# A linear-attention and expert-mixture kernel: another written-out order for its first third, and fewer planned waits for the x block sums

## The chip, the cores and the metric

The kernel runs on one core of a Trainium2 chip. The metric is the device time of one execution in microseconds (us). Three runs of the kernel before took 981.34, 982.95 and 984.04 us; their median, 982.95 us, is the time before. A separate execution was recorded by the profiler, and every duration below is from it.

The engines are called as the profile calls them: PE is TensorE (matrix products; PEld is its weight load), DVE is VectorE, ACT is ScalarE, POOL is GpSimd, and SP is SyncE, which here only starts transfers.

## The reference

```
phi(u) = where(u > 0, u, exp(u) - 1) + 1
kv  = sum over s of phi(k)[s,:] (outer) v[s,:]        per batch and head
x   = phi(q) @ kv / (phi(q) . sum_s phi(k) + 1e-6)    8 batches, 8 heads, 576 x 64
x   = x laid out as 4608 tokens x 512
P   = exp(x @ w_gate - max), 8 rounds of row and column normalisation
out = sum over e of P[:, e] * (relu(x @ w1[e]) @ w2[e])    8 experts, 512 -> 1024 -> 512
```

## The kernel before

**The front.** Sixteen groups of four heads (batch b, half g, group number 2b + g) go through linear attention. For each, k, q and v are loaded from POOL's queue into three buffers each (line 371). ACT takes exponentials (lines 381, 440), DVE forms phi (385, 389 for k, called Kt and Kmin here; 443, 447 for q), PE multiplies k by v (406), and the result is copied out of PSUM (kvz, 333 on DVE or 331 on ACT). PE transposes q (432), the copy out is qpT, PE forms denominators and numerators (463), and DVE writes the product to xT (491), which holds x transposed, 128 partitions by four chunks by 4608 tokens. After every four groups PE computes logits (508).

**The experts.** Tokens are cut in nine blocks of 512, experts and blocks in units. For expert 0 the first layer of the early blocks is plain (677) and the second too (925). From block 5 of expert 0 on, the first layer is a seven-product block scheme (803), whose operands are sums and differences: of x (`x_blocks`, lines 719 to 724), of w1 (the four W operations, 975), and for the second layer (1043) of w2 (the four T operations, 989) and of the hidden values (the four S operations, 1014). ACT and DVE turn products into hidden values (825 to 841). DVE adds second-layer products, scaled by the routing weights P_sb, to the output sums (1074). ACT and POOL do so for one product in seven (1081, 1084). Expert 0's outputs are scaled later, by P_sb, on ACT, DVE or POOL (893), because P_sb comes from eight rounds of normalisation (called Sinkhorn here, 534 to 565) that start only after the last logits. Each round holds a sum on DVE, a small product on PE (549) and a short step on DVE.

**x blocks.** For each of the nine token blocks three tasks form sums of x quarters: the first has two instructions, the others one. They may run on DVE or on POOL. The result is written to DRAM from SP's queue (736), the raw x too (704, 705), and experts 1 to 7 read both back (754). The first five blocks use one output buffer, acc6, as scratch.

**Weights.** w1 and w2 of an expert are loaded by POOL (306) into two buffers each, so w1 of expert 2 overwrites w1 of expert 0. w2 of experts 1 to 7 is one transfer of 1024 KB as stored, w1 two of 512 KB.

**What sets the order.** Nothing is emitted at once: every piece of work is a task with a cost for each engine that may run it, with priority, dependencies and buffer groups, added to a `_Plan`. `_Plan.run` then plays all tasks through a model of the engines and emits each when it is picked, so the plan decides only the order on each engine and which engine runs a task. The semaphore waits come from the data. At the start it follows a list, `_FRONT`, without choosing. A token such as `598g` is task 598 on POOL; p is PE, a is ACT, d is DVE, g is POOL, s is SP, m is a transfer's landing and n is bookkeeping. The list before has 1,506 tasks and ends at 1549p. After its end the model picks the earliest task, by priority. The order of PE's blocks in expert units is also a written chain. A task number is the same in both kernels, because tasks are added in the same sequence. Engines run their instructions in order, so an instruction that waits holds up all behind it on its engine, and on POOL that includes the issue of loads.

Tasks that the steps below name: 444g loads v of group 13, 450p is its k-v product; 472g and 478p are the same for group 14; 498g, 330g and 356g load q of 15, v of 9 and q of 10. 562g, 557g and 569g are x sums. 525p is the last logits product, 492p and 493d the last numerator and the last write of xT in the new order, 528d and 529p the sum and the product of the first Sinkhorn round, 552d its last step (P_sb). 737d to 740d are W, 741d to 744d are T of expert 0; 1011d to 1014d are T of expert 1, 1542d to 1545d T of expert 2. 598g and 1535g load w2 of experts 1 and 2, 1529g and 1531g load w1 of expert 2 in halves. 732g, 734g and 699g scale outputs of expert 0. 992p is the last block with w1 of expert 0, 1043d forms hidden values (841) in the first unit of expert 1, and 1044p is the PE block that reads what 1043d frees. 1405p, 1465p and 1468p are second-layer blocks at the end of expert 1 and the beginning of expert 2.

The lines that the change touches besides the list are the two places in `x_blocks` where a task is given dependencies on landed loads, and the lists that hold these.

Of the kernel before, what the change touches and what calls it, by code (L numbers as in the profile page):

```python
# [17 lines left out]
class _Plan:  # L18
# [121 lines left out]
    1n 108n 119n 601n 48s 49m 2p 3p 50g 51m 4p 0g 5p 6p 52g 53m 7p 8p 76g 77m 9p 78g 79m 10p 54a 11p 80g 81m 12p 13p  # L140
    14p 15p 126g 127m 16p 17p 18p 128g 129m 19p 20p 21p 61n 62a 63d 22p 23p 55d 24p 25p 26p 56d 27p 154g 155m 28p 29p
    30p 64d 130g 131m 31p 57n 32p 33p 109g 110m 58p 111g 112m 65p 59d 34p 66d 35p 36p 37p 89n 82a 60a 156g 157m 38p
    83d 90a 39p 67p 40p 84d 41p 68a 158g 159m 91d 85n 69p 92d 86p 70a 114g 115m 42p 87d 43p 44p 88d 93p 133d 116g
    117m 139n 132a 71a 45p 72p 94d 140a 73d 95p 182g 183m 134d 96a 74p 75d 97p 135n 184g 185m 98a 141d 136p 142d 99a
    186g 187m 46p 137d 143p 161d 138a 47p 160a 102p 144d 113n 120g 121m 602p 103d 145p 603p 146a 162d 100p 210g 211m
    604p 101d 147p 605p 163n 212g 213m 164p 214g 215m 118n 240g 241m 195n 167n 168a 169d 148a 170d 149a 171p 165d
    172d 166a 152p 173p 153d 606p 174a 608p 607d 150p 175p 151d 610p 188a 242g 243m 612p 609d 614p 176a 189d 123g
    124m 616p 615a 190d 196a 618p 197d 104g 105m 191n 177a 192p 198d 617d 611a 199p 193d 613a 620p 194d 122n 244g
    245m 200d 180p 621a 638n 622p 181d 619a 106g 107m 201p 217d 178p 202a 624p 179d 216a 223n 270g 271m 203p 225d
    639p 224a 218d 641p 268g 269m 219n 204a 226d 220p 205a 640d 300g 301m 227p 642d 643p 221a 228d 253n 246a 298g  # L150
    299m 645p 222d 247d 644a 206p 229p 207d 647p 230a 248d 646a 208p 125n 272g 273m 623p 209d 254a 302g 303m 231p
    255d 625p 630d 232a 249n 326g 327m 256d 233a 250p 328g 329m 632d 257p 648d 251a 281n 252a 628p 258d 282a 236p
    259p 237d 649p 260a 283d 234p 284d 261p 311n 274a 626p 235d 262a 651p 275d 650a 263a 285p 276d 354g 355m 266p
    653p 286d 384g 385m 277n 304a 267d 238p 312a 654d 278p 313d 305d 239a 627p 279a 306d 382g 383m 280a 652a 333d
    287p 330g 331m 264p 288a 672p 265d 307n 289p 314d 308p 290a 634d 339n 332a 674p 309d 310d 291a 315p 334d 412g
    413m 292p 659p 316d 358g 359m 340a 341d 356g 357m 317p 293d 629p 318a 414g 415m 342d 360a 294p 671n 319p 673d
    335n 660p 361d 320a 676p 675a 295d 496g 497m 388a 343p 416g 417m 336p 344d 636a 667d 321a 296p 386g 387m 337d
    367n 338d 657p 297a 362d 368a 322p 369d 345p 395n 323d 678p 346a 370d 677a 324p 347p 363n 325d 396a 658p 389d
    364p 348a 555d 349a 371p 665d 655p 390d 679a 562g 372d 661p 365a 425n 366a 419d 373p 352p 397d 374a 680p 353d
    418a 375p 427d 350p 472g 473m 682p 351d 391n 376a 442g 443m 662p 398d 426a 440g 441m 681d 392p 377a 470g 471m  # L160
    420d 556g 399p 428d 393a 656p 394a 400d 683a 380p 498g 499m 401p 381d 684p 402a 663d 378p 453n 403p 379d 421n
    686p 404a 685d 454a 422p 704n 687d 447d 429p 423a 444g 445m 405a 688p 557d 468g 469m 430d 705p 669a 500g 501m
    424d 503d 446a 406p 563g 431p 407d 707p 432a 448d 502a 408p 690p 409d 449n 708a 433p 455d 450p 434a 456d 706d
    435a 510n 457p 451d 689p 481n 458d 452a 505g 558s 559m 438p 696a 459p 439d 709p 460a 504d 436p 461p 437d 692p
    506n 462a 475d 710a 464p 693p 564d 463a 512d 565s 566m 691p 567s 568m 511a 465d 410p 474a 569g 513d 466p 711p
    483d 411a 467d 482a 514p 476d 507p 712a 515d 477n 713p 508a 570g 509a 715p 714d 516p 571d 484d 478p 517a 572s
    573m 560s 561m 698a 518p 479d 700a 717p 519a 574s 575m 694p 716a 480a 485p 520a 521p 486d 695p 522d 487p 719p
    583d 488a 576g 523p 720a 745n 489p 524d 721p 702a 718d 490a 494p 727p 491a 722p 577g 495d 728p 729a 492p 746p
    578g 493d 748p 584d 553n 747a 585d 735d 784g 725p 579s 580m 749a 586s 587m 741d 525p 581s 582m 742d 750p 743d
    526a 588s 589m 527n 737d 726p 751a 528d 785g 752p 733a 723p 753a 786g 754p 738d 739d 756p 842g 755a 787s 788m  # L170
    740d 529p 724p 757a 744d 530d 758p 531d 760p 759a 590g 843g 731a 591n 597n 554p 791n 761a 792p 794p 793a 762d
    766p 844g 795a 763d 532p 768p 767a 764d 592g 593m 798p 533d 772p 534d 594g 595m 789s 790m 845s 846m 847s 848m
    799a 769a 806p 1015s 1016m 773a 800p 802p 796p 776p 801d 797a 803d 807a 770p 777d 535p 810p 536d 812p 765d 808p
    813a 537d 804p 809a 816p 805a 778p 811a 850p 771a 596n 774p 779a 817d 851a 538p 814p 849n 539d 818p 815d 854p
    819a 900g 856p 855a 824p 820d 821d 864p 825a 866p 822d 865a 830p 775d 867a 901g 540d 870p 868p 871a 828p 869a
    902g 857a 874p 852p 872p 823d 853a 826p 873d 831a 860p 827d 541p 858p 861d 834p 875d 862p 835d 876p 863a 542d
    832p 958g 877a 859d 829a 908p 878d 836p 909a 879d 912p 1007d 907n 914p 913a 833d 922p 915a 959g 910p 880d 923a
    884p 543d 911a 918p 837a 960g 916p 882p 598g 599m 903s 904m 905s 906m 1072s 1073m 924p 961s 962m 883a 919d 928p
    963s 964m 925a 917d 888p 885a 1008d 929a 920p 881d 889a 930p 544p 921a 932p 931d 892p 933d 890p 893d 1009d 926p
    894p 545d 927a 600n 891d 934p 546d 966p 886p 967a 895a 970p 965n 935a 972p 968p 973a 936d 980p 969a 940p 887d  # L180
    971a 937d 547p 974p 981a 938d 942p 941a 939d 976p 943a 548d 944p 975d 977d 946p 945a 549d 986p 947a 982p 987a
    950p 983a 990p 984p 951d 948p 991d 988p 949d 550p 992p 551d 978p 989d 952p 979a 1528n 552d 1000p 953a 1006n 1017n
    1010d 697g 985a 1018p 1020p 1019a 1001p 668g 1021a 1024p 1005d 1026p 633g 1025a 1011d 1022p 993a 1028p 1012d 840a
    998p 955g 1027d 956a 999p 1013d 1023a 701g 1029d 631a 996p 1014d 1030p 664g 1004d 1032p 1031a 635d 1034p 637a
    994p 1529g 1530m 1033a 1531g 1532m 995p 1035a 838a 732g 1038p 1040p 1039a 1036p 670a 1041d 1042p 1075p 1037a
    1043d 1077p 1076a 1002d 997p 1078a 1044p 1003d 1074n 1534n 1081p 1045a 1129s 1130m 1535g 1536m 1083p 896g 1082a
    1046d 1079p 1050p 1047d 1052p 1048d 1051a 1533n 730a 1049d 1055p 1080a 1053d 1054d 1085p 1060p 1086d 699d 1063p
    1062d 734d 1087p 839d 1089p 1088a 1061d 1091p 1084d 1090a 1066p 1092a 1058a 1095p 1537n 1067d 1097p 703d 1096a
    1093p 1065d 1056a 1099p 1098d 1094a 1057g 1132p 1068d 666a 1134p 1100d 1069p 1133a 1135a 1101p 1070d 1131n 1138p
    1064d 1102a 1186s 1187m 1140p 1071d 1136p 1103d 1107p 1104d 1109p 1105d 1108a 1139a 1106d 1112p 1110d 1142p 1111d  # L190
    1115a 1117p 1137a 1143d 1116g 1120p 1059g 1118d 782d 1144p 1119d 1146p 1141d 1145a 1148p 1122d 1147a 1123p 1149a
    957a 1152p 1125d 1154p 1124d 1153a 1150p 1155d 1156p 1151a 1189p 1157d 1191p 1190a 1121d 1126p 1192a 1158p 1128d
    1188n 1195p 1127d 1159a 1243s 1244m 1197p 1196a 1160d 1193p 1113a 1164p 1198d 1194a 1161d 1166p 1165a 1162d 1169p
    1163d 1199p 1168d 1172a 1174p 1167d 781a 1173g 1200d 954a 1177p 1114g 1176d 1175d 1201p 1203p 1205p 1204a 1180p
    1206a 1202a 1209p 1182d 1211p 1179d 1210a 1207p 1178d 1170a 1213p 736d 783a 1171g 1246p 1181d 1208a 1248p 1214d
    897g 1183p 1247a 1249a 1215p 1185d 1245n 1252p 1184d 1216a 1300s 1301m 1254p 1212d 1253a 1250p 1217d 1221p 1218d
    1223p 1222a 1219d 1226p 1220d 1224d 1256p 1227a 1225d 1231p 1251a 1228g 1257d 1229a 1234p 899g 1232d 1255d 1258p
# [18 lines left out]
def kernel(  # L216
# [20 lines left out]
    NG = N // 512  # L237
# [7 lines left out]
    add = S_.add  # L245
# [83 lines left out]
    def copy(e, dst, src):  # L329
# [4 lines left out]
        else:  # L334
            nc.gpsimd.tensor_copy(out=dst, in_=src)

    w_part, wg_done = {}, []
    front_ids = []
    xt_done = {}
    gates = {}  # L340
    v_land, all_land, kv_id, t_id = [], [], [], [None]

    def fadd(*a, **kw):
        t = add(*a, **kw)
        front_ids.append(t)
        return t

# [854 lines left out]
```

## Time and profile before

| what | value |
|---|---|
| runs | 981.34, 982.95, 984.04 us |
| span of the profiled execution | 982.6 us, 0.35 under the runs' median |
| PE busy | 954.4 us (97%) |
| DVE busy | 792.4 us (81%) |
| ACT busy | 575.2 us (59%) |
| POOL busy | 198.6 us (20%) |
| bytes read from HBM, written | 119.69 MB, 17.69 MB |

How to read it: busy shares are means over the span. The page cuts the span in 40 slices of 24.6 us and shows each engine's busy tenths, and PEclk, the share of the clock that PE was granted. A table of stretches gives, for each, its length, then busy time and number of instructions for PE, PEld, DVE, ACT and POOL, the granted clock, the transfer engines' busy share and GB/s. A line of waits reads: who waited, for what, total us, times, longest. A line of the order of time reads: start, us, engine, line, operation, output and inputs with sizes, how many in a row; in brackets, idle time before it and what ended that. A line of transfers ends in the median us from issue to landing. "us" of a matmul group includes its drain, so successive starts say more than durations.

### The profile page before, as it was taken

To read this page: it belongs to the slowest core of one execution; us is meant where nothing else is said; L and a number is where in the kernel's file an instruction comes from. 1 tells how busy PE (TensorE), PEld (TensorE's weight loads), DVE (VectorE), ACT (ScalarE), POOL (GpSimd) and SP (SyncE) were. 2 spreads that over 40 slices of the span, in tenths; PEclk is the share of its full clock that TensorE was granted. 3 is DMA by queue.
4 is the path that set the end of the run, shared out by engine and by line. 5 is a ranking of instruction groups with operands and counts; after the bars stand their busy time and mean duration, and the time that the engine had idled before them with its cause. 6 is when DMAs were issued, how large, how long until landed. Compare 5 with 4: busy or idle time off the path is not lost.

```text
span 982.6 us, 21104 instructions
## 1 busy us (share of the span) xinstructions
PE 954.4 (97%) x8576; PEld 806.4 (82%) x8576; DVE 792.4 (81%) x1471; ACT 575.2 (59%) x1025; POOL 198.6 (20%) x247
## 2 busy tenths in 40 slices
PE   8998988999998999999999999999999999999998
PEld 4555557878887888888888888888888888888886
DVE  7998699887877788878888788878888788877775
ACT  6897645566554555555555555555555555555552
POOL 6443355152112111121112111121112111111110
PEclk9999999999999999999999999999999999999999
DMA  9996372462213522272224522272224422235554
GB/s 222 258 255 145 113 209 86 72 126 78 77 72 108 130 75 76 77 161 76 76 76 116 122 76 76 76 162 75 76 77 120 117 77 76 76 97 162 162 161 108
DMA packets 45682, 112.52 MB, mean 115 GB/s; under 512 B 4369, under 2 KB 25617, under 8 KB 45585
## 3 DMA queue, kind: packets, MB, share of 16 engines
q1 hardware_dynamic: 21056, 75.57, 23.5%
q0 software_dynamic: 24128, 35.07, 19.0%
q8 instruction: 67, 1.10, 0.4%
q10 hardware_dynamic: 400, 0.52, 0.2%
q14 instruction: 31, 0.25, 0.1%
HBM read 119.69 MB, written 17.69 MB: 140 GB/s over the span
## 4 chain that ended last, share of the span: by engine, by line
PE 80%; DVE 2%; issue 0%; ACT 0%; DVEq 0%; ACTq 0%
PE ye L1043 34%; PE hq L803 23%; PE R L803 11%; PE Zye L803 6%; PE Zye L1043 6%; PE ye L925 1%; DVE T L989 1%; DVE h L841 0%; DVE acc L1074 0%; PE yc L909 0%; DVE W L975 0%; DVE acc L1061 0%; DVE xT L1014 0%; ACT st L1081 0%; DVE acc L943 0%
## 5 line engine op out<-in xcount | busy, mean ns | idle before, releaser
L1074 DVE SCALAR_TENSOR_TENSOR acc<-ye,P_sb,acc 128x256 f32<-128x256 f32 x620 | 268.0, 478 | 128.1 <-PE ye L1043 127.0
L803 PEld LDWEIGHTS <-W 128*128 128x128 f16 x2144 | 210.0, 98 | 24.8
L1084 POOL TENSOR_TENSOR acc<-acc,st 128x256 f32<-128x256 f32 x124 | 89.6, 741 | 618.3 <-ACT st L1081 606.4
L1043 PEld LDWEIGHTS <-S 128*128 128x128 f16 x1984 | 194.1, 98 | 23.1 <-issue 0.7
L1043 PE MATMUL ye<-T,S 128*128 128x256 f16 x1488 | 192.8, 273 | 0.0
L803 PEld LDWEIGHTS <-w 128*128 128x128 f16 x1608 | 157.5, 98 | 20.3 <-issue 1.1
L1043 PEld LDWEIGHTS <-h 128*128 128x128 f16 x1584 | 155.3, 98 | 22.1 <-issue 3.8
L838 ACT ACTIVATE h<-hq 128x512 f16<-128x512 f32 x134 | 80.1, 598 | 154.8 <-PE hq L803 153.7
L803 PE MATMUL hq<-xs,W 128*128 128x256 f16 x1008 | 151.4, 273 | 0.0
L803 PE MATMUL R<-xs,W 128*128 128x256 f16 x1008 | 151.2, 273 | 0.0
L803 PE MATMUL hq<-xs,w 128*128 128x256 f16 x1008 | 141.4, 273 | 0.7 <-DVE h L841 0.7
L835 ACT ACTIVATE h<-Zye 128x512 f16<-128x512 f32 x134 | 80.0, 597 | 41.8 <-PE Zye L803 41.6
L841 DVE CUSTOM_DVE_ANT_0 h<-R,s 128x512 f16<-128x512 f32 x126 | 86.5, 686 | 13.1 <-ACT s L825 12.6
L1081 ACT ACTIVATE st<-Zye,P_sb 128x256 f32<-128x256 f32 x124 | 52.8, 471 | 74.9 <-PE Zye L1043 74.9
L1014 DVE TENSOR_TENSOR S<-h 128x1024 f16<-128x1024 f16 x124 | 85.7, 691 | 11.5 <-ACT h L838 11.3
L825 ACT COPY s<-hq 128x512 f32<-128x512 f32 x126 | 73.5, 584 | 35.0 <-PE hq L803 34.7
L818 ACT COPY Zye<-hq 128x512 f32<-128x512 f32 x134 | 77.9, 581 | 23.9 <-PE hq L803 23.5
L841 DVE CUSTOM_DVE_ANT_0 h<-hq,s 128x512 f16<-128x512 f32 x126 | 86.5, 687 | 3.1 <-PE hq L803 2.5
L803 PE MATMUL Zye<-xs,w 128*128 128x256 f16 x504 | 75.6, 273 | 0.0
L832 ACT COPY s<-R 128x512 f32<-128x512 f32 x126 | 74.6, 592 | 0.0
L1043 PE MATMUL ye<-T,h 128*128 128x256 f16 x496 | 65.1, 275 | 3.7 <-DVE acc L1074 3.7
L1043 PE MATMUL ye<-w,h 128*128 128x256 f16 x528 | 68.4, 273 | 0.0
(120 smaller groups left out, 1038.6 us busy)
## 6 DMA issues: line engine op xcount, KB each, us to landing
xs<-xd SPq DMA_DIRECT2D x63, 896.0 KB, 4.6
kin<-in_k_dram POOLq DMA_DIRECT2D x15, 576.0 KB, 8.8
out_dram<-acc SPq DMA_DIRECT2D x67, 128.0 KB, 2.4
w<-in_moe_w_dram POOLq DMA_DIRECT2D x16, 512.0 KB, 8.4
w<-in_moe_w_dram POOLq DMA_DIRECT2D x7, 1024.0 KB, 13.2
qin<-in_q_dram POOLq DMA_DIRECT2D x16, 288.0 KB, 8.1
vv<-in_v_dram POOLq DMA_DIRECT2D x16, 288.0 KB, 8.5
xd<-acc SPq DMA_DIRECT2D x5, 512.0 KB, 3.0
```

Of the source, the lines that this page charges most:

```text
L803: nc.tensor.matmul(dst[:, p, :], lhsT=lhs(p, c), rhs=rhs(c), start=(first and p == 0 and c == 0), stop=(c == 1), skip_group_check=True)
L818: nc.scalar.copy(out=Zt[1], in_=gX["tile"])
L825: nc.scalar.copy(out=gs2["tile"], in_=gX["tile"])
L832: nc.scalar.copy(out=gs5["tile"], in_=gR["tile"])
L835: nc.scalar.activation(out=hd(0, 0), in_=Zt[1], func=AF.Relu)
L838: nc.scalar.activation(out=hd(1, 0), in_=gX["tile"], func=AF.Relu)
L841: nc.vector._custom_dve(TENSOR_ADD_SAT, out=dst, in0=ps, in1=sb, s0=3.0e38, s1=0.0)
L1014: nc.vector.tensor_tensor(out=Sx[:, i], in0=a0, in1=a1, op=op)
L1043: nc.tensor.matmul(bank(g_)[:, s, :], lhsT=lhs(s, kk), rhs=rhs(kk), start=(new and s == 0 and kk == 0), stop=(kk == 3), skip_group_check=True)
L1074: nc.vector.scalar_tensor_tensor(out=dst(), in0=bank(g_)[:, s, :], scalar=P_sb[:, gg, e:e + 1], in1=dst(), op0=ALU.mult, op1=ALU.add)
L1081: nc.scalar.mul(out=gst["tile"], in_=bank(g_)[:, s, :], mul=P_sb[:, gg, e:e + 1])
L1084: nc.gpsimd.tensor_tensor(out=dst(), in0=dst(), in1=gst["tile"], op=ALU.add)
```

## The change

Three things. First, `_FRONT` is another list: 1,733 tasks instead of 1,506, all of the old ones and 227 more, ending at 1706d instead of 1549p. The set of tasks and their data are unchanged; the order on each engine changes, and many tasks with a choice change engine. Of the 27 x sums, 13 are on POOL instead of 20. Second, the first five blocks' sums are no longer planned behind the landing of a v load. Third, their stores are no longer planned behind the landing of all loads. The second and third are dependencies of the plan, between tasks that share no data.

```
-    v_land, all_land, kv_id, t_id = [], [], [], [None]
+    kv_id, t_id = [], [None]
...
-        v_land.append(tin["v"])
-        all_land.extend(tin.values())
...
-                       deps=deps + [v_land[NG + 1 + g] if early else t_close, last] +
+                       deps=deps + [None if early else t_close, last] +
...
-        ti = add(("sp", 0.45), f_st, deps=[last] + all_land, use=[gt_], prio=0.0)
+        ti = add(("sp", 0.45), f_st, deps=[last], use=[gt_], prio=0.0)
```

Of the list, the lines that matter below, before (-) and after (+). The v load of group 13 and its use, the T operations of expert 0, and the first Sinkhorn round:

```
-    686p 404a 685d 454a 422p 704n 687d 447d 429p 423a 444g 445m 405a 688p 557d 468g 469m 430d 705p 669a 500g 501m
-    424d 503d 446a 406p 563g 431p 407d 707p 432a 448d 502a 408p 690p 409d 449n 708a 433p 455d 450p 434a 456d 706d
...
-    578g 493d 748p 584d 553n 747a 585d 735d 784g 725p 579s 580m 749a 586s 587m 741d 525p 581s 582m 742d 750p 743d
-    526a 588s 589m 527n 737d 726p 751a 528d 785g 752p 733a 723p 753a 786g 754p 738d 739d 756p 842g 755a 787s 788m
-    740d 529p 724p 757a 744d 530d 758p 531d 760p 759a 590g 843g 731a 591n 597n 554p 791n 761a 792p 794p 793a 762d
...
+    577g 396a 371p 677d 363n 364p 372d 679a 349a 398d 656p 444g 445m 365d 418a 440g 441m 680p 366d 663d 352p 373p 353d
...
+    510n 511a 472g 473m 431p 456d 408p 690p 505g 432a 409d 704n 708a 691p 448d 706a 503d 433p 449n 450p 434a 570d 696a
...
+    482a 572s 573m 712d 574s 575m 713p 476d 508a 509a 702a 741d 715p 581s 582m 714a 483d 516p 742d 477n 478p 517a 716d
...
+    523p 489p 524d 746p 490a 743d 494p 491a 721p 744d 748p 745n 747a 495d 728p 749d 492p 750p 493d 722p 553n 737d 751a
+    784d 525p 729a 738d 785g 752p 526a 735a 528d 725p 753a 754p 786d 554p 755a 739d 527n 529p 787s 788m 756p 588s 589m
```

The x sums 562g, 557g and 569g in the new list:

```
+    562g 205a 227p 221d 639p 222d 228d 246a 206p 641p 207d 638n 640a 104g 105m 229p 247d 642a 208p 268g 269m 643p 209d
...
+    288a 657p 265d 384g 385m 289p 634d 358g 359m 307n 308p 290a 333d 557g 332a 315p 309d 659p 310d 654a 316d 442g 443m
...
+    446a 421n 422p 447d 470g 471m 578d 569g 405a 429p 423d 579s 580m 689p 424d 560s 561m 430a 406p 707p 407d 567s 568m
```

The weight loads 598g, 1529g and 1531g (in the old list 1529g and 1531g stand after 1018p, 598g long before):

```
-    884p 543d 911a 918p 837a 960g 916p 882p 598g 599m 903s 904m 905s 906m 1072s 1073m 924p 961s 962m 883a 919d 928p
...
+    989d 992p 730a 952p 949d 1528n 1529g 1530m 1019a 1020p 732g 953a 1024p 1006n 1021a 1000p 1025a 734g 1026p 1022p
+    1028p 699g 1017n 1023a 998p 1029d 993a 668a 666d 597n 598g 599m 999p 781d 635a 1531g 1532m 1030p 1004d 1001p 1031a
+    631g 703d 1032p 1034p 840g 1033a 994p 945d 1005a 637d 1038p 897g 995p 1039a 1027d 1035a 633d 996p 1002a 600n 1011d
+    1040p 1036p 1012d 1042p 1037a 1075p 1043d 664a 1077p 1013d 997p 1076a 1078a 1041d 1044p 670a 1014d 1081p 1129s
```

The load 1535g and the first T of expert 2; 1542d to 1545d are not in the old list, whose end is shown first:

```
-    1043d 1077p 1076a 1002d 997p 1078a 1044p 1003d 1074n 1534n 1081p 1045a 1129s 1130m 1535g 1536m 1083p 896g 1082a
...
-    1462p 1461d 1460d 1486p 1483d 1488p 1490p 1489a 1465p 1491a 1487a 1494p 1466d 1496p 1495a 1492p 1497d 1498p 1493a
-    1549p
...
+    1341a 1348p 1347d 1342g 1369d 1372p 1534n 1535g 1536m 1346d 1374p 1373a 1541d 1376p 956g 1375a 1351p 1377a 1380p
...
+    1427p 1391d 1402p 1428d 1405p 1537n 1542d 1403d 1429p 1404d 1431p 1407d 1430a 1433p 1426d 1432a 1408p 1434a 1437p
```

## The prediction

> **What bounds the kernel now.** I read the page's busy lines, then busy time by stretch, then TensorE's (PE's) waits, then the order of time around the longest.
>
> ```profile
> PE   8998988999998999999999999999999999999998
> DVE  7998699887877788878888788878888788877775
> ```
>
> PE is busy nearly everywhere; only the first third of the span has slices below 9. The stretches that I cut:
>
> ```profile
> core 0: us, PE busy (x) PEld busy (x) DVE busy (x) ACT busy (x) POOL busy (x), PEclk, DMA share, GB/s
> 0.00:124.60 124.60, 112.41 (x966) 63.83 (x967) 103.44 (x163) 96.60 (x128) 56.17 (x77) 0.99 0.85 196
> 124.60:191.60 67.00, 60.30 (x528) 48.94 (x527) 63.92 (x117) 33.43 (x63) 23.27 (x19) 0.97 0.53 134
> 191.60:207.10 15.50, 15.03 (x106) 10.11 (x104) 10.93 (x17) 11.71 (x21) 12.63 (x9) 1.00 0.18 27
> ...
> 300.00:320.00 20.00, 16.33 (x137) 13.97 (x136) 13.71 (x27) 9.27 (x18) 5.49 (x7) 0.91 0.40 94
> 320.00:982.60 662.60, 657.96 (x6002) 586.95 (x6000) 523.68 (x1005) 369.52 (x692) 83.59 (x118) 1.00 0.36 102
> ```
>
> From 320 us on PE idles 4.6 us in 662.6, most of it at the very end; nothing is to be won there. Between 124.6 (last logits) and 191.6 (last expert-0 block of line 803) VectorE (DVE) is busy 63.9 of 67.0 us and sets the pace. Both lists run the same PE work before task 1044p (207.1 us before) and again before 1465p (301.3 us). So **only idle PE time and half-clock time can change**. In the first 208 us PE's order of time shows 17.5 us of gaps over 0.15 us. PE's waits after 90 us:
>
> ```profile
> PE ye L1043 <- DVE acc L1074: 4.2, 2, 3.7
> PE R L549 <- DVE gs L544: 3.3, 1, 3.3
> PE kv_ps L406 <- DMA vv<-in_v_dram: 2.6, 1, 2.6
> ```
>
> Each long gap is paid twice, in idle time and in a slow clock behind it:
>
> ```profile
> 96.40:99.80 3.40, 3.40 (x18) 2.04 (x18) 1.24 (x3) 0.95 (x2) 1.77 (x3) 0.50 0.03 5
> 308.10:311.50 3.40, 2.92 (x15) 2.08 (x15) 1.30 (x4) 0.17 (x1) 0.00 (x0) 0.50 0.00 0
> ```
>
> PEclk is 0.50 in both. The gaps of 2.60, 3.29 and 3.67 us were each followed by such a 3.4 us stretch; those of 1.44, 1.63 and 1.78 us were not. PE works in some 3.2 us of a stretch at half speed: 1.6 us lost (1.5 at 308). The Trainium skill ("TensorE: Matmul & The Clock Gate", Part 1) asks for a whole idle window of about 3.4 us before the clock halves; the trace differs, since 2.60 sufficed. By that rule the first two gaps below would return no clock time and the sum would be 3.2 us smaller.
>
> **Part by part.** Durations are rows of the profiled execution (span 982.6 us, 0.35 below the runs' median of 982.95). A position is PE work listed ahead: 0.44 us per four-matmul block, 0.87 per eight, as successive starts show.
>
> *The late v load, 95.49 us.* 444g (v of group 13) waited on POOL 5.71 us for KV work, was issued at 87.79 and landed 7.6 us later. Its distance from issue to use (450p) is 4.5 us of PE work in the old list, 15.3 in the new, where 478p, now the last group, has 14.9. Load rows take 4 to 13 us from issue to landing, so the cover holds: 2.60 + 1.6 = **-4.2**. If another load is late instead: 0.
>
> *The shared port, front.* A POOL sum stretches DVE operations with two SBUF inputs:
>
> ```profile
> 160.69 0.68 DVE L1014 TENSOR_TENSOR xT<-h,xT 128x1024 f16<-128x1024 f16 x1
> ...
> 167.88 1.64 DVE L975 TENSOR_TENSOR W<-w 128x1024 f16<-128x1024 f16 x1
> ```
>
> ```profile
> 165.81 1.60 POOL L720 TENSOR_TENSOR xst<-xT 128x512 f16<-128x512 f16 x1
> 167.38 1.60 POOL L722 TENSOR_TENSOR xst<-xT,xst 128x512 f16<-128x512 f16 x1
> ```
>
> The same shape takes 0.68 alone and 1.64 beside POOL. Over all rows DVE loses 18.0 us so, 6.6 before 124.6 and 8.4 from there to 191.6; copies out of PSUM lose nothing. The old list has 20 of 27 x sums on POOL, the new 13. In the new one 562g, 557g and 569g have kvz copies out of PSUM next on DVE; the old one put 784g and 786g beside T and W. Two gaps hang on stretched operations: 1.78 at 72.53 (behind a Kmin, line 389, of 2.51 instead of 0.76) and 1.44 at 118.95 (behind a sum of 2.68 instead of about 0.8). I take **-3.2**; bounds 0 and -3.2. Before 55 us I take nothing: k and v of group 6 landed at 40.1 and 45.6, their uses started at 41.7 and 46.7, and the new list has nearly the same loads ahead.
>
> *Sinkhorn's first sum, 134.16 us.* 529p waits 3.29 us for 528d, queued behind T and W operations of 1.5 to 1.6. The new list moves 741d to 744d ahead of the logits. Left are W, a sum and W between the last xT (493d) and 528d: 0.75 + 0.68 + 0.8 + 1.0, then 3.1 for 528d itself, against 5.8 us of PE work from 492p's end: with hand-overs 529p is some 1.0 late. 3.29 - 1.0 + 1.6 = **-3.9** (bounds -1.6, -4.9).
>
> *DVE-bound stretch.* POOL's x sums fall from 21.4 us here (their rows added up) to 8.5 (four single sums of 1.48, a pair of 2.55); at 8.4/21.4 of stretch per us DVE gets back some 5 us. The gaps of 0.78, 0.99 and 1.63 (155 to 170 us) hang on it; I take half, **-1.7** (bounds 0, -3.4). A new order brings small stalls of its own; the old one's that I have not named come to 1.1 us between 28 and 190 us: I take **+1.5** (bounds 0, +6).
>
> *The w2 load of expert 1: a new wait.* This is what speaks against the change. Before:
>
> ```profile
> 170.48 0.94 POOL L306 DMA_DIRECT2D w<-in_moe_w_dram  x1
> 193.26 9.81 POOL L893 TENSOR_SCALAR acc<-acc,P_sb 128x512 f32<-128x512 f32 x6 [21.84 <-DVE P_sb L565]
> 203.01 1.30 POOL L306 DMA_DIRECT2D w<-in_moe_w_dram  x2
> ```
>
> 598g was issued at 170.5 and used by 1011d at 196.3. The new list puts it on POOL behind 1529g (w1 of expert 2, which overwrites expert 0's w1 and so waits for 992p), 732g, 734g and 699g. From 992p's end: 0.1, 0.65, then three scales of 1.6: 598g goes out 5.6 us later. Its landing:
>
> ```profile
> w<-in_moe_w_dram POOLq DMA_DIRECT2D x1, 1024.0 KB, 12.5
> ```
>
> Other 1024 KB loads took 12.8 to 15.0, beside other traffic; two halves issued together 8.5. I take 11.5: it lands at +17.1. 1011d waits there, with 1012d and 1043d (0.7 each) queued behind, and 1044p needs 1043d: +19.2, against 13.9 us of PE work. Idle 5.3, less the 0.34 that this place had before, plus 1.6 of clock: **+6.6** (landing at 8.5: 2.0 without a clock drop; at 15.0: 10.1).
>
> *The end of the list.* The old list ends at 1549p. The T of expert 2, not in it, then came in a row, among the h operations that PE waited for:
>
> ```profile
> 303.99 0.68 DVE L989 TENSOR_TENSOR T<-w 128x1024 f16<-128x1024 f16 x1
> 304.59 0.68 DVE L841 CUSTOM_DVE_ANT_0 h<-hq,s 128x512 f16<-128x512 f32 x1
> 305.19 0.82 DVE L989 TENSOR_TENSOR T<-w,T 128x1024 f16<-128x1024 f16 x1
> ```
>
> The new list has 1542d to 1545d one per unit from about 287 us on, and ends mid-expert, where such operations come one per unit in the old run without a gap: 3.67 + 1.5 = **-5.2**. But 1535g (w2 of expert 2) now stands 11.8 us of PE work ahead of 1542d (before, 96 us of time); at 12.9 to landing the evictions behind 1542d are late: **+1.0** (bounds 0, +3.9).
>
> Stores of x blocks move forward (558s at position 55 instead of 84); loads around them have 7.5 us of PE work or more from issue to use, a 512 KB store row takes 3: nothing. The waits dropped in the code are the planner's alone.
>
> **Sum:** -4.2 - 3.2 - 3.9 - 1.7 + 1.5 + 6.6 - 5.2 + 1.0 = -9.1: span 973.5, run 973.9.
>
> **Rivals.** *B, w2 in time.* If 598g lands within 6 us, its stall and that of 1542d go: -16.7, 966.3. For: 512 KB landed in 5.8. Against: every 1024 KB row. The Trainium skill ("DMA: Bandwidth & Descriptors", Anatomy of one DMA) gives 2.0 us plus bytes over 436 GB/s, an estimate of 4.4 for 1024 KB, which would make this rival come true; no row agrees.
>
> *C, the front gives it back.* DVE and ACT are both busy over 90% from 40 to 70 us, so a stall removed can return one task later. With a quarter of the front's -13.0 left: -3.2 + 6.6 - 5.2 + 1.0 = -0.8, 982.2 (979 to 985.9).
>
> *D, slower: loads bound the front.* POOL issues in order. The new list has six x sums ahead of the last load, 3 x 2.55 + 3 x 1.48 = 12.1 us; the old two, 4.0. If the load queue runs empty, each makes all later loads late: +8.1 instead of -7.4 up to the logits, so +6.4, 989.4. It decides once landing takes longer than issue to use; the least distances are 7.5, 8.6 and 8.7 us of PE work, the load rows there 4 to 10. Against: queued loads hide a pause.
>
> **Numbers.** Forecast (970 to 979) 0.52, B 0.12, C 0.25, D 0.11. Range 965 to 984, which leaves out D and the edges of B and C. A measurement tells about 0.3% from no change: faster (below 980.0) 0.52 + 0.12 + 0.05 = 0.69, slower (above 985.9) 0.12, the rest 0.19.
>
> **What would show it.** No DMA-released PE gap at 450p; 529p's wait near 1 us; no gap where 1468p stood at 308.58; a gap of about 5 us ahead of 1044p, with DVE idle before line 989 and released by the DMA of w, and PEclk 0.5 behind it. If that gap is under 2 us, B is right; if PE waits on k, q or v landings between 55 and 110 us, D.

## The result, and the profile after

The changed kernel takes **971.08 us** in the median of 4 runs (969.86 to 973.25), beside 982.14 us for the kernel before on the same chip: a ratio of 0.988, 95% interval 0.985 to 0.991. Forecast were 973.9 us and a range of 965 to 984. The profiled execution ran 969.86 us, with a span of 967.8. The time is inside the range; the steps are only half right, and the experiments below say which.

The page of the changed kernel, busy tenths of PE and the granted clock in 40 slices of 24.2 us:

```profile
PE   8999999999999999999999999999999999999998
PEclk9999999989999999999999999999999999999999
```

Before, PE had five slices below 9 among the first thirteen; now only the first of them is. The single dip of the clock, in the ninth slice, is new. Stretches cut at the same tasks as before (last logits, 992p, 1044p); columns are length, busy time of PE, PEld, DVE, ACT and POOL, granted clock, transfers' busy share, GB/s:

```profile
0.00:117.70 117.70, 111.09 (x966) 62.92 (x967) 100.54 (x166) 99.22 (x130) 57.33 (x78) 1.00 0.98 224
117.70:177.30 59.60, 59.31 (x535) 49.20 (x534) 56.42 (x122) 38.43 (x71) 7.98 (x6) 1.00 0.30 100
177.30:196.00 18.70, 14.15 (x99) 9.49 (x98) 8.58 (x15) 10.88 (x20) 11.70 (x9) 0.95 0.74 112
```

The front took 124.6 us and takes 117.7. From the last logits to 992p it was 67.0 with DVE busy for 63.9; it is 59.6, and PE now sets its pace (59.3 busy). POOL's work there fell from 23.3 to 8.0 us. The third stretch is longer, 18.7 instead of 15.5 us, and PE idles in 4.5 us of it. Line numbers below the list are higher now, by 10 up to the forming of phi(k) (306 is 316) and by 8 behind that (803 is 811, 841 is 849, 549 is 557). The wait of 3.7 us at 1468p is gone, and so is that of 3.3 at 529p, whose row has no bracket now:

```profile
121.81 0.36 PE L557 MATMUL R<-gs,ones_t 128*128 128x8 f32 x2
```

A wait of 4.5 us ahead of 1044p is the new wait of the forecast. POOL's order of time, the load's landing, and DVE's and PE's order of time show its steps:

```profile
177.81 0.64 POOL L316 DMA_DIRECT2D w<-in_moe_w_dram  x1 [24.49 <-PE hq L811]
178.49 4.85 POOL L901 TENSOR_SCALAR acc<-acc,P_sb 128x512 f32<-128x512 f32 x3
183.29 1.62 POOL L316 DMA_DIRECT2D w<-in_moe_w_dram  x2
```

```profile
w<-in_moe_w_dram POOLq DMA_DIRECT2D x1, 1024.0 KB, 10.6
```

```profile
193.87 0.69 DVE L997 TENSOR_TENSOR T<-w 128x1024 f16<-128x1024 f16 x1 [6.42 <-DMA w<-in_moe_w_dram]
...
195.21 0.68 DVE L849 CUSTOM_DVE_ANT_0 h<-hq,s 128x512 f16<-128x512 f32 x1
```

```profile
195.94 1.01 PE L811 MATMUL hq<-xs,w 128*128 128x256 f16 x4 [4.54 <-DVE h L849]
```

POOL issues half of w1 of expert 2, does three scales, and only then issues w2 of expert 1 (598g, 183.29 us). It lands 10.6 us later, DVE stands 6.42 us at T with an h operation behind, and PE idles 4.54 us. The granted clock after it, in stretches of 3.4 us:

```profile
194.00:197.40 3.40, 1.46 (x8) 1.00 (x8) 3.37 (x6) 0.41 (x1) 0.00 (x0) 0.50 0.16 30
197.40:200.80 3.40, 3.40 (x17) 2.34 (x16) 2.21 (x4) 1.24 (x3) 0.00 (x0) 0.50 0.74 268
200.80:204.20 3.40, 3.40 (x33) 3.05 (x32) 2.21 (x5) 2.17 (x4) 0.66 (x1) 1.00 0.02 7
```

Two stretches at 0.50: PE gets through 17 operations in 3.40 us, then 33.

### The profile page after: what moved, and what is told of

It reads as the page before. It is cut to its first block, busy times and chain, and to the rows that moved or that the text cites. A ratio compares the mean times of both kernels' runs of the same rounds, so it can differ in the third digit from the quotient of the medians.

```text
span 967.8 us, 21113 instructions
## 1 busy us (share of the span) xinstructions
PE 952.0 (98%) x8576; PEld 805.4 (83%) x8576; DVE 780.3 (81%) x1476; ACT 578.9 (60%) x1029; POOL 184.7 (19%) x238
## 4 chain that ended last, share of the span: by engine, by line
PE 78%; DMA 2%; DVE 0%; issue 0%; ACT 0%; ACTq 0%
PE ye L1051 33%; PE hq L811 22%; PE R L811 11%; PE Zye L811 6%; PE Zye L1051 6%; DMA w<-in_moe_w_dram 1%; DMA xs<-xd 1%; PE ye L933 1%; PE yc L917 0%; DVE h L849 0%; ACT st L1089 0%; DVE T L997 0%; DVE acc L1082 0%; DVE acc L922 0%; ACTq L1089 0%
## 5 line engine op out<-in xcount | busy, mean ns | idle before, releaser
L1051 PE MATMUL Zye<-w,h 128*128 128x256 f16 x528 | 68.4, 272 | 0.0
```

Of the source, the lines that this page charges most:

```text
L1051: nc.tensor.matmul(bank(g_)[:, s, :], lhsT=lhs(s, kk), rhs=rhs(kk), start=(new and s == 0 and kk == 0), stop=(kk == 3), skip_group_check=True)
```

## The experiments

With the list of before, the changed code gives the order of before on all five engines, instruction by instruction. So the dropped dependencies do nothing by themselves. They permit the new list, which the plan cannot follow with them in place; all of the difference in time lies in the order. Edits are shown as tokens of the list.

### Both kernels again

Unedited. The changed kernel:

> The changed kernel, unedited, as the base for the three kernels beside it. Its ratio to the kernel before was 0.988; expected 0.985 to 0.991, one PE gap of 4.5 us ahead of 1044p, and the granted clock at 0.5 for 6.8 us behind it.

Measured: 971.09 us (4 runs), ratio 0.989 (0.987 to 0.991); a gap of 4.42 us ahead of 1044p and 6.83 us at half clock.

The kernel before, twice (after the experiments on its list, below):

> The kernel before, unedited, profiled once more. The kernel with only its T operations moved late in the list has the same order up to 284 us, and showed no gap at 450p, where the profile of before had 2.60 us behind a transfer. Theory A (the gap belongs to one execution): 450p's gap is under 0.5 us here, the product starts near 93.4 us, and one of the three half-clock stretches is gone. Theory B (the gap belongs to the kernel): 2.2 to 2.6 us again.

> As the run ahead of it, a third execution of the kernel before: theory A gives a gap at 450p in some executions and not in others, with the landing of v of group 13 varying by 2 us or more; theory B 2.2 to 2.6 us in all. The gaps at 324p (1.78), 494p (1.44), 529p (3.29) and 1468p (3.67), which no transfer releases, are expected within 0.1 us of these in all executions.

Measured: 981.46 and 979.98 us, spans of 979.7 and 978.2, against 982.6 in the profile that I forecast from. The load of v of group 13, in each of the two from issue to landing, and PE's order of time there:

```profile
vv<-in_v_dram POOLq DMA_DIRECT2D x1, 288.0 KB, 6.2
```

```profile
93.81 0.92 PE L406 MATMUL kv_ps<-vv,t 64*128 64x192 f16 x18 [1.26 <-DMA vv<-in_v_dram]
```

```profile
vv<-in_v_dram POOLq DMA_DIRECT2D x1, 288.0 KB, 4.8
```

With a landing of 7.6 us the gap was 2.60 us in the first profile; with 6.2 it is 1.26, and with 4.8 there is none (450p starts at 93.40 us without a wait). The last logits begin at 124.62, 121.75 and 121.86 us. So the gap belongs to the execution, as theory A had it, though A's bound of 0.5 us was missed in the first of the two. From the second denominator product (69p) to the last logits it takes 110.5 us in the first profile, 107.9 with the gap of 1.26 us, and 107.0 without one: of the 1.26 us some 0.9 stayed, and waits behind it shrank by the rest. The four gaps that are released by an engine and that the forecast named (1.78, 1.44, 3.29 and 3.67 us) are within 0.1 us of each other in all executions of this order. A smaller one is not: 466p waited 0.28 us for DVE in the first of the two and 1.34 in the second. Nor are the half-clock stretches. Those two gaps of 3.29 and 3.67 us, with the 3.4 us behind each, in the last execution:

```profile
128.10:131.40 3.30, 0.01 (x2) 0.04 (x1) 3.16 (x6) 0.60 (x1) 3.22 (x4) 1.00 0.40 125
131.40:134.80 3.40, 3.40 (x18) 1.74 (x19) 3.33 (x7) 1.27 (x3) 1.49 (x3) 1.00 0.67 166
301.80:305.50 3.70, 0.04 (x1) 0.00 (x0) 3.65 (x7) 1.15 (x3) 1.72 (x2) 1.00 0.01 2
305.50:308.90 3.40, 3.39 (x32) 3.03 (x32) 2.13 (x5) 1.59 (x3) 1.30 (x2) 1.00 0.29 57
```

PE is idle in the first and third line and at full clock in the second and fourth. Neither gap cost any clock here; in the execution before it each cost one such stretch, and the last section says why. The two stretches were not worth the same. With the one behind 1468p, the time from 1465p to the last products is 1.4 us longer. With the one behind 529p, the time from the last logits to 992p is only 0.3 us longer (66.45 against 66.19 us), though PE works through 3.4 us at half the clock: DVE sets the pace there, and where PE ran at full clock, 532p and 768p waited 0.65 and 0.21 us for it.

### The v load, exchanged with another

```diff
- 427d 350p 472g 473m 682p ... 429p 423a 444g 445m 405a
+ 427d 350p 444g 445m 682p ... 429p 423a 472g 473m 405a
```

> The kernel before, with two loads exchanged in its list: v of group 13 (444g) goes out where v of group 14 (472g) stood, some 13 us earlier, and the other way round. Theory: the 2.60 us gap ahead of 450p and the clock at 0.5 for 3.413 us behind it go, and v of 14 still lands in time for 478p at 110: 4.2 us less than the kernel before up to 529p. Rival 1: DVE and ACT are over 90% busy in the front, so the stall comes back at the next task that waits for them: less than 2 us gained. Rival 2: the gap goes, 529p's sum is late all the same because DVE sets its time, and only the clock's 1.7 us is gained.

> The kernel with the loads of v of groups 13 and 14 exchanged, profiled once more: no gap at 450p in this execution either (its load goes out some 13 us earlier), and 525p and 529p as late as in the undisturbed executions of the kernel before, near 122 and 131.5 us, since nothing else in that stretch was moved. Rival: the transfer wait shows up at 478p or at 466p instead.

Measured: 981.93 us (12 runs) beside 982.89, ratio 0.9992 (0.9980 to 1.0004): under 2.0 us gained, if any. The load goes out at 75.7 and 75.8 instead of 87.8 us, no gap stands at 450p in either profile and no transfer wait at 478p or 466p (466p waited for DVE, 1.75 and 1.35 us), and 525p begins at 122.27 and 122.00 us, no sooner than in the two later executions of the kernel before. The forecast of 4.2 us failed. Rival 1's bound held, but not for its reason alone: of the five profiled executions that have the old order up to 450p, two had a gap of over 2 us there (2.60 and 2.21), one 1.26, and two none.

### The front's sums taken apart

```diff
- 390d 679a 562g ... 719p 583d 488a ... 748p 584d 553n 747a 585d
+ 390d 679a 562d ... 719p 583g 488a ... 748p 584g 553n 747a 585g
```

> The kernel before, with the front's two pairs of sums that ran side by side taken apart: 562 from POOL to DVE (POOL's sum stretched a Kmin to 2.51 us), and 583, 584 and 585 from DVE to POOL (583 took 2.68 us on DVE beside POOL's). Theory of the shared port, front: the gap of 1.78 us at 72.5 shrinks by 1.75 less the 0.84 that the sum takes on DVE, and that of 1.44 at 119 goes: 1.4 to 3.2 us less than the kernel before, if 528d does not wait. Rival: DVE sets the front's end, so that the gaps go and 529p waits as much longer: within 1 us.

Measured: 979.56 us (12 runs) beside 982.55, ratio 0.9965 (0.9951 to 0.9978): 3.4 us less (2.2 to 4.8). The gaps of 1.78 us at 72.5 and 1.44 us at 119 are gone, for one of 0.57, and 529p does not wait longer but less:

```profile
128.95 0.36 PE L549 MATMUL R<-gs,ones_t 128*128 128x8 f32 x2 [1.91 <-DVE gs L544]
```

1.91 us instead of 3.29: the sums 584 and 585, now on POOL, were part of DVE's queue ahead of 528d. So the theory holds in size, but not all of the 3.4 us arose in the front: from the second denominator product to the last logits it takes 105.8 us here, against 107.0 and 107.9 in the two later executions of the kernel before. The step of 562 is the clean test. Its sum went onto the busier engine, and Kmin took 0.76 us instead of 2.51 and the gap closed all the same. That of 583 is less clean, since DVE was rid of the sum itself and not only of its lengthening. ("Shared port" is the forecast's name for that lengthening; the runs show the lengthening and not what is shared.)

### The T operations of expert 0, put back

```diff
- 715p 581s ... 477n 478p ... 494p 491a ... 748p 745n ... 784d 525p 729a
+ 784d 525p 741d 742d 743d 744d 729a
```

The upper line had 741d, 742d, 743d and 744d ahead of those four pairs.

> The changed kernel, with the four T operations of expert 0 (741d to 744d) moved from ahead of the last logits to right behind 525p, between it and the first Sinkhorn sum 528d, as the kernel before had three of them. Theory: 528d, which is just in time in the changed kernel (it ends 0.15 us ahead of 529p), comes 4 times 0.6 = 2.4 us later, 529p waits 2.4 us, and the clock may fall to 0.5 behind it (it did behind 2.60 and not behind 1.78): 2.4 to 4.1 us more than the changed kernel's 971.1. Rival: the T were not what made the difference, because W and the sums ahead of 528d, or the shared port, set its time: less than 1 us.

Measured: 974.24 us (6 runs, 973.33 to 979.68), 3.15 more than the unedited changed kernel; ratio to the kernel before 0.992 (0.990 to 0.995).

```profile
125.71 0.56 PE L557 MATMUL R<-gs,ones_t 128*128 128x8 f32 x2 [2.88 <-DVE gs L552]
```

Expected were 2.4 us. One of the four ran beside a POOL sum (1.52 instead of 0.68 us), and a half-clock stretch followed, so 529p's round came 2.9 us later with respect to the logits, and the next one 4.0. The rival, less than 1 us, falls.

### Seven sums, back on POOL and in the old list off it

In the changed kernel:

```diff
- 784d 786d 842d 844d 900d 959d 960d
+ 784g 786g 842g 844g 900g 959g 960g
```

> The changed kernel, with seven x sums of blocks 5 to 8 that it runs on DVE (784, 786, 842, 844, 900, 959, 960) put back on POOL, where the kernel before had them, at the same places of the list. Theory of the shared port: DVE operations with two SBUF inputs that run beside them take 1.5 to 1.6 us instead of 0.7, some 0.42 us of stretch for each of about 11 us of sums, 4 to 5 us in all between 110 and 180 us, against about 6 us of work taken off DVE; PE's gaps there come back for 2 to 5 us, and 992p starts that much later. Rival: the order alone did it, DVE is rid of as much work as it is stretched, and 992p starts within 1 us of where it was.

In the kernel before, the same seven the other way (g to d):

> The kernel before, with seven x sums of blocks 5 to 8 (784, 786, 842, 844, 900, 959, 960) on DVE instead of POOL, at the same places of the list: the mirror image of the kernel in which they were put back. Theory of the shared port: DVE gets some 4 us of sums more and is rid of 5 to 7 us of stretch (9.2 us between 120 and 195 us before), so that 529p's gap of 3.29 and those of 0.78, 0.99 and 1.63 shrink: 1.5 to 4 us less than the kernel before. Rival: the sums displace just what DVE was late with (528d, T, S), and the time stays within 1 us or grows.

Measured: 975.73 us (6 runs), 4.64 more than the changed kernel, ratio to before 0.994 (0.992 to 0.995); and 980.47 us (12 runs) beside 982.89, ratio 0.998 (0.997 to 0.999), 2.2 us less (1.0 to 3.3). The same S operation (line 1022), in the changed kernel's order of time on DVE, and then with the sums on POOL:

```profile
141.13 0.69 DVE L1022 TENSOR_TENSOR xT<-h 128x1024 f16<-128x1024 f16 x1
```

```profile
142.33 1.66 DVE L1022 TENSOR_TENSOR xT<-h 128x1024 f16<-128x1024 f16 x1 [0.19 <-POOL xst L727]
```

It takes 1.66 us instead of 0.69, and a W operation (983) 1.64 instead of 0.68. Between 120 and 195 us such lengthening adds up to 7.5 us instead of 2.9 with the sums on POOL (in the old list to 5.2 instead of 9.2 with them off it), though DVE has fewer sums to do. Gaps of 0.78 at 529p, 0.58 and 0.65 come back, and 992p starts 2.6 us later. In the old list the wait at 529p went from 3.29 to 0.03 us, but 2.24 us came back at 532p one round later, and the stretch from the last logits to 992p became only 1.5 us shorter: DVE still set the pace. Both theories hold, in both directions. The rival, that the order alone did it, falls, in the old list narrowly (it allowed up to 1 us).

### The w2 load, earlier

All 25 us of it, and then one scale of 1.6 us only:

```diff
- 873d 958g 832p ... 668a 666d 597n 598g 599m 999p
+ 873d 958g 597n 598g 599m 832p ... 668a 666d 999p
```

```diff
- 1028p 699g 1017n ... 598g 599m 999p
+ 1028p 1017n ... 598g 599m 699g 999p
```

> The changed kernel, with the load of expert 1's w2 (598g) moved ahead in the list, to right behind the x sum 958g, some 25 us earlier on POOL's queue. Theory: the 4.54 us gap ahead of 1044p stands on the issue of this load alone, and the clock at 0.5 for 6.83 us behind it (worth about 2.4 to 3.4 us) on the gap; both go, so 6.5 to 7.5 us less than the changed kernel, some 964 us. Rival 1: something else holds the T operations or h there (the h operations of the block before, POOL's scales), so DVE waits for that in place of the DMA: less than 1.5 us gained. Rival 2: the gap goes and the clock falls to 0.5 in the same place all the same, so that the gap was not what caused it: 4.2 us gained.

> The changed kernel, with one of the three 1.6 us scales that stand ahead of 598g on POOL (699g) moved behind it. Theory: the load goes out 1.6 us earlier, lands 1.6 us earlier, and the gap ahead of 1044p shrinks by the same, 4.54 to about 2.9 us; the clock still falls to 0.5 behind it, for 3.4 or 6.8 us, as it did behind 2.60 us in the kernel before; 1.6 us less than the changed kernel with the same drop of the clock, 2.8 to 3.3 us less with half of it. Rival: the load's landing is set by the traffic beside it, not by its issue, and the gap stays within 0.5 us of 4.54.

Measured, the first: **963.52 us** (4 runs, 961.75 to 964.81), ratio to the kernel before 0.981 (0.979 to 0.983), 7.6 us less than the changed kernel. The start of 1044p in PE's order of time, without a bracket, and the stretch up to 196 us:

```profile
193.19 0.60 PE L811 MATMUL hq<-xs,w 128*128 128x256 f16 x4
```

```profile
179.00:196.00 17.00, 17.00 (x127) 12.18 (x125) 12.62 (x20) 12.68 (x23) 10.91 (x8) 1.00 0.48 77
```

No gap, PE busy for 17.00 of 17.00 us, clock 1.00 where it was 0.95. Neither rival holds. Between the unedited changed kernel and this one, the time from 992p to 1044p is 4.58 us shorter, that from 1044p to 1123p 2.68 (the half clock), and what follows within 0.4. It is the fastest version of all.

In this execution the stretch from the second denominator product to the last logits took 105.6 us, against 103.3 to 104.3 in the five other executions with this order of the front. The two instructions of 569g, on POOL from 86.48 to 88.76 us, met another DVE operation than in the others. The same operation, in the profile of the changed kernel and then here:

```profile
85.46 0.75 DVE L455 TENSOR_TENSOR tq<-tq,eq 128x1152 f16<-128x1152 f16 x1
```

```profile
85.88 3.50 DVE L455 TENSOR_TENSOR tq<-tq,eq 128x1152 f16<-128x1152 f16 x1
```

PE then waited 2.32 us at 422p, a gap that none of those five has. In the other five, 569g made an operation of line 395, which has one tensor as input, take 1.71 us instead of 0.74.

The second: 969.22 us (4 runs, 967.46 to 969.81), 1.9 less than the changed kernel. The load goes out one scale earlier and the gap is 3.11 instead of 4.42 us:

```profile
196.47 0.60 PE L811 MATMUL hq<-xs,w 128*128 128x256 f16 x4 [3.11 <-DVE h L849]
```

The gap shrinks by 1.3 for 1.6 us: the landing follows the issue, and the rival (0.5 us) falls. One half-clock stretch follows instead of two, worth 1.0 us by the time from 1044p to 1123p; together 2.3 us where I expected 2.8 to 3.3, since of the unedited kernel's two stretches the first held 1.3 us of the gap.

### The end of the list

```diff
- 1428d 1405p 1399g ... 1435p 1441p 1436a ... 1483d 1488p 1490p
+ 1428d 1405p 1542d 1399g ... 1435p 1441p 1543d 1436a ... 1483d 1488p 1544d 1490p
```

> The kernel before, with its list lengthened at one point only: the T operations of expert 2 (1542d, 1543d, 1544d) written in behind 1405p, 1441p and 1488p, one per unit, instead of coming in a row after the list's end. Theory (end of the list): the 3.67 us gap ahead of 1468p at 308.58 us and the clock at 0.5 for 3.413 us behind it go, 5.2 us less than the kernel before (ratio 0.9945 to 0.995). Rival: DVE owes the same work in any order there, the gap turns into small ones, or comes back behind the new end of the written part: within 1.5 us of the kernel before.

Measured: 978.17 us (6 runs) beside 982.89, ratio 0.9956 (0.9938 to 0.9973): 4.3 us less (2.7 to 6.1). The gap ahead of 1468p is smaller, not gone, and no half clock follows:

```profile
303.75 1.03 PE L1043 MATMUL ye<-T,h 128*128 128x256 f16 x8 [1.59 <-DVE acc L1074]
```

From 1465p to the last products it takes 661.16 us, against 664.60 and 663.24 in the two later executions of the kernel before, with and without half clock behind that gap. 1545d and the seams beyond the new end stayed with the planner. The step holds, and the rival (1.5 us) falls; its size here is a little under the 5.2 forecast.

## Why the prediction came out right, step by step

From the execution of the kernel before at 981.46 us to that of the changed one at 970.31 (spans 979.7 and 968.4), task starts give: 4.6 us less from the second denominator product to the last logits, 2.4 less from there to 1465p, 4.8 less from 1465p to the last products, and 0.5 more at both ends together. Sum -11.3, forecast -9.1.

**The late v load, -4.2: wrong.** I read a wait behind a transfer in one profile as a property of the kernel. Over executions of one and the same order the landing took 4.8 to 7.6 us and the gap was 0 to 2.60; the exchange of the loads gained 0.8 us (-0.4 to 2.0). Some 3.5 us was to be had in the profiled execution (110.5 us against the 107.0 of the undisturbed one), and little in most.

**The base was one of the longer executions.** Every run takes 1.7 to 2.2 us more than its span, so a span of 982.6 stands for some 984.5 us, well over the median. The profile held three half-clock stretches; over half of the runs, by their mean clock, hold fewer. This error and the one above are the same accident: a base too long by some 2 us, and a step that promised to take it away. The forecast also added only 0.4 us to its span of 973.5 to get a run of 973.9; at 1.7 to 2.2 us it would have been some 975.4, and farther from the result.

**The shared port in the front, -3.2: right in size.** Without a load gap in either, that stretch is 3.4 us shorter (107.0 to 103.6), and taking apart the front's sums alone gained 3.4, of which 1.2 to 2.0 in the front itself. That 562g, 557g and 569g would have only copies out of PSUM beside them was wrong: 569g lengthened an operation of line 395 by 1.0 us, and in one execution one of line 455 by 2.75.

**Sinkhorn's first sum, -3.9: wait right, clock wrong.** I expected 529p 1.0 us late. 528d ends 0.15 us ahead of it: the wait went entirely, -3.3. Putting the T operations back cost 3.15. The 1.6 us of clock in this term was not to be had in the old order. The forecast itself said that DVE sets the pace there, and so the half clock behind 529p was worth 0.3 to 0.4 us: to 992p it takes 66.45 to 66.62 us in the five executions of this order with it, and 66.19 in the one without.

**The DVE-bound stretch, -1.7 + 1.5: the term that was mis-sized.** All three gaps (0.78, 1.01, 1.64) went, -3.4 and not half, and the small stalls that I set against them came to 0.3, not 1.5. The stretch up to 992p took 66.5 us and takes 59.2. From the last logits to 1044p it took 82.2 to 82.5 us, and takes 73.5 in the version without the w2 stall: 8.7 to 9.0 less, where this term and the one above promised 4.1. These nearly 5 us are what made up for the v load. How they divide over single gaps is not shown.

**The w2 load, +6.6: right, by other parts.** The gap is 4.5 us (forecast 5.3), since the load landed in 10.4 to 10.6 us (11.5 taken); the clock cost 2.7 (1.6). Less the 0.34 of before, +6.8; taking it away gained 7.6. Rival B priced this at 966.3 and its condition never arose; the early load made it true, at 963.5.

**1542d behind 1535g, +1.0: wrong, nothing.** 1535g goes out at 266.16 us and lands 9.5 us later; 1542d runs at 277.37 without a wait.

**The end of the list, -5.2: right.** From 1465p on -4.8; the old list with three T operations alone, -4.3 (-6.1 to -2.7).

Rival C, that the front gives its gain back, fell for the change as a whole: 3.4 to 4.6 us went in the front and 8.7 to 9.0 behind it, where the forecast had 13.0 together. Single repairs in the old list were given back in part: 466p waited for DVE where 450p no longer did, and 532p where 529p no longer did. Rival D, that loads bound the front, fell: the front's waits of PE for transfers are those for w, 1.3 us in two.

So the sum was right to about 2 us by luck: a step that is not there in most executions (4.2) and a stretch that was undervalued (nearly 5) cancelled. What was shown by experiment: the w2 load, the lengthening beside POOL's sums in both stretches, the T operations, the end of the list. Only read from traces: that 528d's remaining margin is 0.15 us, the worth of the half clock behind 529p, and the fate of the small gaps.

## What to carry to other kernels

Profile the kernel before more than once before pricing its waits: its four large gaps that an engine releases came back to 0.1 us in every execution of one order, a gap that a transfer released did not (0 to 2.60 us), nor did two that waited for DVE in the crowded front (0 to 1.34 us at 466p in the old order, 0 to 2.32 at 422p in the new). A half-clock stretch is to be priced only where PE sets the pace: it was worth 1.4 us in one place and 0.3 in another. After a list has been searched anew, look for loads that it has put behind compute on the queue that issues them: moving one token here gave 7.6 us on top of the 11 of the whole new list. Where the operations of two engines lengthen each other, moving work to the idle one can be worse than doing it on the busy one: seven sums moved to the idle engine cost 4.6 us.

## What the runs showed of the hardware

**What a gap costs in clock depends on where it falls.** In the first profile the half-clock stretches begin at 96.43, 133.97 and 308.05 us: 11.0 and 62.0 times 3.413 apart. In each execution all clock changes lie on such a grid, whose start differs (4.3 to 7.2 us after the span's). Cut on that grid, every stretch of 3.413 us after the first 35 us in which PE idled for 2.1 us or more was followed by one at half clock (18 of 18), in 14 executions of ten kernels; of those with 1.0 to 2.0 us, six were (three of these at half clock themselves) and over thirty were not. The gap of 3.29 us was followed by half clock where it took 2.1 to 3.2 us of one stretch, and not in the execution where the grid split it into 1.45 and 1.84; so with 3.67, split into 1.79 and 1.88. The 4.54 us gap fell into two stretches (2.58 and 1.96) and both were followed by half clock; one of 4.84 took 0.9, 3.41 and 0.5 of three, and only the second was:

```profile
200.70:204.10 3.40, 2.92 (x14) 2.02 (x14) 3.37 (x6) 1.65 (x3) 0.00 (x0) 0.50 0.23 38
204.20:207.60 3.40, 3.40 (x33) 3.05 (x32) 1.99 (x5) 1.47 (x4) 0.00 (x0) 1.00 0.57 233
```

(This is the changed kernel with its T operations put back.) The forecast held the length of a gap against the Trainium skill's idle window ("TensorE: Matmul & The Clock Gate", Part 1). The traces agree with its free-running window of about 3.4 us, and differ in that the window need not be wholly idle: 2.1 of 3.4 us sufficed.

**The runs come in steps.** 50 runs of the kernel before, by their mean granted clock:

| mean clock | runs | time |
|---|---|---|
| 0.999 | 6 | 980.0 to 980.3 us |
| 0.995 to 0.997 | 22 | 981.3 to 983.0 us |
| 0.993 to 0.994 | 22 | 983.0 to 986.2 us |

Between the medians a step is 1.7 and 1.9 us. The profiled executions show what lies under the first: that at 0.999 (979.98 us) has no half-clock stretch, that at 0.995 (981.46 us) has the two behind 529p and 1468p, worth 0.3 and 1.4 us. The first profile, at 0.994, has a third, behind the late v load. A kernel without long gaps has none of these steps: the version with the early load has a mean clock of 0.999 or 1.000 in all its runs. They spread over 961.75 to 964.81 us all the same, for which the clock cannot be the reason; the lengthened operation of line 455 is one that its profile shows.
